# An RWKV attention with mixture-of-depths kernel: whole v tiles, quarter state products, and a new order of stores, weights and one batch's expert work

## The chip, the cores and the metric

The kernel runs on one core of one Trainium2 chip. The metric is the device time of one execution in microseconds (us). All times below come from three runs of the kernel before the change and from one profiled execution of it.

## The reference

The inputs r, k and v have 4 batches, 8 heads, 768 tokens and 48 channels a head. A decaying state runs over the tokens of each batch and head; its output y is then the input of a mixture-of-depths block, which sends the 128 best-scored tokens of each batch through a two-layer expert.

```python
for t in range(S):
    cur = einsum('bhd,bhe->bhde', u * k[t], v[t])
    y[t] = einsum('bhd,bhde->bhe', r[t], state + cur)
    state = w * state + einsum('bhd,bhe->bhde', k[t], v[t])
x = y as (B, S, H * D)                    # 4 x 768 x 384
scores = x @ w_gate
out = x
for b in range(B):
    top = the 128 tokens of batch b with the highest scores
    out[b, top] = x[b, top] + sigmoid(scores) * (relu(x[b, top] @ w1) @ w2)
```

w1 is 384 x 1024 and w2 is 1024 x 384. All is in float32.

## The kernel before

**Units.** A unit n is 128 tokens of one batch, so a batch has NC = 6 units and there are NU = 24. Within a unit two halves of C = 64 tokens are treated as chunks: inside a chunk the sum over earlier tokens is a masked matrix of scores (rows of the page: L259 scores, L302 the masked copy into `at`, L226 and L234 its diagonal), and between chunks a state of 48 x 48 a head is carried (Z0, Z1, G; `states` and `decays`). The output y of a unit is the sum of `from_state` (z times rh) and `from_values` (at times v); both are rows of L287.

**The main loop** (pass i, 0 to 24; its line numbers are in the listing) works on three units at once. On TensorE a pass issues, in this order: y from the states of unit i-1; the scores of unit i; in passes called *late* the state products of unit i (L269); y from the values of unit i-1; the transposes of k and r of unit i+1 (L240, into the PSUM tiles `pt` and `ea` or `st`); in passes not late the state products of unit i (L282, tile `st`); pieces of the expert's matrices if some are queued (`hidden` L467, `expert` L477); one transpose of a column of scores (L369); and, when no expert work is queued, three matmuls that nobody reads (L264), written into a part of the next unit's `rp` tile. A pass is late when the expert's queue is not empty at its start.

VectorE does the masked copy, the state sums, the product rh (L245), the bonus sum `du` (L219) and the ranks of tokens. ScalarE copies y out to x (L330, L331), copies k's transpose (L250), and makes the first half of the diagonal (L226) and the decays (L318). GpSimd (POOL) makes the second half of the diagonal (L234), then for unit i+2 the scaled k (`scaled`, L209) and the bonus products (`bonus`, L213 and L215), then what is to be gathered or scattered (L417, L508).

**The transfers.** All loads and the stores of x are issued by SP, in the order in which the loop writes them: in pass i k and r of unit i+4 (192 KB each, 1024 runs of 192 B), v of unit i+3 in two halves (96 KB each), `weights(WEIGHTS.get(i, 0))` pieces of w1 (128 KB) or w2 (192 KB), then the store of unit i-2. A store waits for ScalarE's copy of its unit. Both halves of v lie in one tile with a dimension of two chunks; what belongs to the other chunk is zero, so that one matmul over 128 tokens gives the state sums of both chunks side by side. The zeros are written once by `clear_v`, for each of the six v buffers, on POOL, ScalarE or VectorE.

**The expert's work.** When batch b's last unit e has left, pass e+3 ranks its tokens, makes a one-hot matrix, picks the 128 indices (`pick`, L405 and L409) and gathers their rows from the output in HBM (`fetch`, L417, by POOL). The gather waits for all stores of this batch. In pass e+4 `chosen` transposes the gathered rows (L434) and copies them (L436), and `enqueue` puts 8 pieces of `hidden`, 8 of `expert` and a `leave` into the queue; `share(i)` spreads them over the following passes. `at` places each of these at a named place of a pass, and `run` calls what stands there. The last batch is done after the loop.

The lines that hold the order are these:

```python
b, c = divmod(n, NC)                      # load_v: two halves
for j in range(2):
    rows = slice(c * T + j * C, c * T + (j + 1) * C)
    nc.sync.dma_start(out=vins[n % NV][half(j), :, j, :], in_=v[b, :, rows, :]...)
WEIGHTS = {i: 1 for i in range(3, 9)} | {9: 3, 10: 3, 11: 3, 12: 3, 13: 2}
```

Of the kernel before, what the change touches and what calls it, by code (L numbers as in the profile page):

```python
# [7 lines left out]
F32 = mybir.dt.float32  # L8
# [9 lines left out]
def kernel(  # L18
# [13 lines left out]
    nc = tc.nc  # L32
# [29 lines left out]
    nc.vector.memset(tiny, 0.0)  # L62
    zero = const.tile([128, 1], F32)
    nc.vector.memset(zero, 0.0)
    one = const.tile([1, 128], F32)
# [5 lines left out]
    kws = [const.tile([128, H, PAD], F32, name=f"kw{i}") for i in range(NKW)]  # L71
    vins = [const.tile([128, H, 2, D], F32, name=f"vin{i}") for i in range(NV)]
    KIN = {}

    def half(j):
        return slice(j * C, (j + 1) * C)
# [11 lines left out]
    def load_v(n):  # L88
        b, c = divmod(n, NC)
        for j in range(2):  # L90
            rows = slice(c * T + j * C, c * T + (j + 1) * C)
            nc.sync.dma_start(out=vins[n % NV][half(j), :, j, :], in_=v[b, :, rows, :].rearrange("h t d -> t h d"))

    def clear_v(n):
        for j in range(2):
            o = vins[n][half(j), :, 1 - j, :]
            if n in (2, 3):
                nc.scalar.activation(o, zero[half(j), :, None].to_broadcast([C, H, D]), AF.Copy)
            elif n == 4:
                nc.vector.memset(o, 0.0)  # L100
            else:
                nc.gpsimd.memset(o, 0.0)

# [10 lines left out]
    nc.scalar.activation(tiny[:, 1:2], tiny[:, 0:1], AF.Sigmoid)  # L114
    clear_v(2)
    clear_v(3)

# [13 lines left out]
    tri = const.tile([128, 128], F32)  # L131
    clear_v(4)
    up = const.tile([128, NP, C + 1], F32)
    nc.vector.memset(up[:, :, 0:1], 1.0)
    winv = const.tile([128, 1, NP], F32)

    clear_v(0)
    clear_v(1)
    nc.gpsimd.memset(rpads[1][:, :, D:], 0.0)  # L139
# [50 lines left out]

    WEIGHTS = {i: 1 for i in range(3, 9)} | {9: 3, 10: 3, 11: 3, 12: 3, 13: 2}
    parts = [(q, kd) for q in range(4) for kd in range(KD)] + list(range(FB))
# [12 lines left out]

    KH, RH, RKU, DU, AT, RP, ST, Z0, Z1, G, YP, YS, X = {}, {}, {}, {}, {}, {}, {}, {}, {}, {}, {}, {}, {}

# [53 lines left out]

    def unread(t, m):
        for _ in range(m):
            nc.tensor.matmul(out=t, lhsT=ident, rhs=ident, start=True, stop=True, skip_group_check=True)  # L264

    def state_product(n, hp, i, c):
        if c and n % NC == NC - 1:
            return
        nc.tensor.matmul(out=RP[n][half(i), c, NP * C + hp * D : NP * C + (hp + 1) * D],  # L269
                         lhsT=kws[n % NKW][half(c), 2 * hp + i, :], rhs=vins[n % NV][half(c), 2 * hp + i, c, :],  # L270
                         start=True, stop=True, skip_group_check=True)

    def sums(n, c):
        if n not in ST:
            return RP[n][:, c, NP * C : NP * (C + D)].rearrange("d (p e) -> d p e", p=NP)
        return ST[n][:, : NP * 2 * D].rearrange("d (p c e) -> d p c e", p=NP, c=2)[:, :, c, :]

    def state_products(n):
        m = 1 if n % NC == NC - 1 else 2
        for hp in range(NP):  # L280
            for i in range(2):
                nc.tensor.matmul(out=ST[n][half(i), hp * 2 * D : (hp * 2 + m) * D], lhsT=kws[n % NKW][:, 2 * hp + i, :],  # L282
                                 rhs=vins[n % NV][:, 2 * hp + i, :m, :], start=True, stop=True, skip_group_check=True)

# [12 lines left out]
    def from_values(n, hp, i, c):  # L297
        y_product(n, c, hp, i, AT[n][half(c), i * NP + hp, :], vins[n % NV][half(c), 2 * hp + i, c, :])

# [249 lines left out]
    for b in range(B - 1):  # L549
        e = b * NC + NC - 1  # L550
        at(e + 3, "start", rank, b)
        for z in range(NST):
            at(e + 3, "start", one_hot, b, z)
            at(e + 3, "pick" if b else "chosen", pick, b, z, "pt")
            at(e + 3, "fetch", fetch, b, z)
            at(e + 4, "chosen", chosen, b, z, "pt")
            at(e + 5, "middle", gate_sum, b, z)
            at(e + 6, "gate", gate, b, z)
            at(e + 4, "chosen", enqueue, b, z)

# [17 lines left out]
    def first():  # L578
        RP[0] = psum.tile([128, 2, 512], F32, name="rp")
        for hp in range(NP):  # L580
            for j in range(2):
                for c in range(2):
                    score_product(0, hp, j, c)
        turned(1, turn(rpads[1], "ea"))
        ST[0] = psum.tile([128, 512], F32, name="st")
        state_products(0)
        Z1[0] = work.tile([128, NP, D], F32, name="z1")
        nc.vector.tensor_copy(Z1[0], sums(0, 0))
        diagonals(0)
        masked(0)  # L590
        G[0] = work.tile([128, NP, D], F32, name="g")
        nc.vector.tensor_add(G[0], sums(0, 1), Z1[0])
        turned_k(1, turn(kws[1], "pt"))
        bonus_sum(1)
        diagonals(1)
        nc.vector.tensor_mul(wc, up[:, :, C], up[:, :, C])  # L596
        nc.vector.tensor_scalar(tri, jp, 0.0, None, op0=OP.is_lt)
        nc.scalar.copy(wg, spread(1, "eb"))
        scaled(2)
        bonus(2)  # L600

    for i in range(NU + 1):
        if i + 4 < NU:
            load_kr(i + 4)
        if i + 3 < NU:
            load_v(i + 3)
        weights(WEIGHTS.get(i, 0))
        if i > 1:
            store_y(i - 2)
        late = bool(queue)  # L610
        if not i:
# [14 lines left out]
        if i < NU:  # L626
            if i not in RP:
                RP[i] = psum.tile([128, 2, 512], F32, name="rp")
            for hp in range(NP):
                for j in range(2):  # L630
                    for c in range(2):
                        score_product(i, hp, j, c)
            if late:
                for hp in range(NP):
                    for c in range(2):
                        for j in range(2):
                            state_product(i, hp, j, c)
        else:
# [19 lines left out]
        run(i, "start")  # L658
        if late and i < NU:
            states(i)  # L660
        if i + 1 < NU:
            if i:
                turned_k(i + 1, turn(kws[(i + 1) % NKW], "pt"))
            turned(i + 1, turn(rpads[(i + 1) % NIN], "st" if late else "ea"))
        run(i, "turned")
        old = len(ready)
        leaving()
        if i < NU and not late:
            if i:
                ST[i] = psum.tile([128, 512], F32, name="st")  # L670
            state_products(i)
            states(i)
        m = share(i)
# [13 lines left out]
        if 2 <= i < NU:  # L687
            against_earlier(i - 2)
            score_row(i - 2, None if late or i != NC + 2 else "ea")
            against_own(i - 2)  # L690
        run(i, "last")
        if i + 1 < NU and not queue:
            RP[i + 1] = psum.tile([128, 2, 512], F32, name="rp")
            unread(RP[i + 1][:, 0, 384:], 3)
        run(i, "chosen")
# [3 lines left out]
        if i == 2:  # L699
            clear_v(5)  # L700
        if i == 4:
            numbers()
# [69 lines left out]
```

## Time and profile before

| what | value |
|---|---|
| runs, median (lowest to highest) | 173.16 us (173.14 to 176.85) |
| profiled execution | 172.11 us |
| its span, first to last instruction | 170.3 us |
| mean granted TensorE clock | 0.97 |
| PE busy | 149.1 us (88% of the span) |
| DVE, ACT, POOL busy | 110.4, 97.6, 103.9 us |
| transfers | 24.13 MB, 142 GB/s on average, 93% of the packets under 512 B |
| median time from issue to landing: r, k, v half, store | 5.0, 4.3, 4.0, 3.5 us |
| the same: w1 piece, w2 piece, gather | 3.4, 4.1, 3.7 us |

The profile is a record of one execution. It gives each engine's busy time, a row of 40 slices, the chain of work that ended last, the groups of instructions by source line with what ended the idle time before them, and a timeline of single instructions. PE is TensorE's matmuls, PEld its weight loads, DVE is VectorE, ACT is ScalarE, POOL is GpSimd, SP issues transfers. L234 is line 234. In the chain of waits a line is start, length and what; in the timeline it is start, length, engine, line, operation, what is written and read, the shapes, and in brackets the idle time before it with what ended it. "issue" stands for a wait whose cause the profile does not name.

### The profile page before, as it was taken

Reading aid. Unit: us, or ns where it says so; the run is one execution under the profiler, and the core shown is the slowest. Engines: PE = TensorE matmul, PEld = TensorE weight load, DVE = VectorE, ACT = ScalarE, POOL = GpSimd, SP = SyncE. Lnnn points to the kernel's source line nnn. Section 1 sums busy time; section 2 is a strip of 40 time slices with the busy share of each in tenths; the row PEclk is TensorE's granted clock in tenths of the full one; section 3 lists DMA queues with packets and bytes.
Section 4 is the critical chain, followed back from the end, with each engine's and each line's share of the span. In section 5 each row is a group of like instructions: output and inputs, shape, how many; then the busy total and the mean of one; then the engine's idle time right before and its main releaser. Section 6 shows DMA issues by size and latency. Waiting matters only on the chain.

```text
span 170.3 us, 8282 instructions
## 1 busy us (share of the span) xinstructions
PE 149.1 (88%) x3475; PEld 127.1 (75%) x3475; DVE 110.4 (65%) x315; ACT 97.6 (57%) x346; POOL 103.9 (61%) x138
## 2 busy tenths in 40 slices
PE   5899999999996189996979967999998998997990
PEld 3677888988884179996848766998787797756990
DVE  5679988888980354768378479666975796733000
ACT  6656888886757026475637754875676867401200
POOL 7999998997660792866562696986558331022022
PEclk9999999999999755999999999999999999999999
DMA  3999799866886997678898996898721112112000
GB/s 67 179 187 168 143 175 188 198 144 119 191 199 154 183 214 188 144 178 230 183 233 209 206 198 125 182 220 169 157 98 50 50 52 94 48 18 80 0 20 26
DMA packets 82197, 24.13 MB, mean 142 GB/s; under 512 B 76126, under 2 KB 81792, under 8 KB 82160
## 3 DMA queue, kind: packets, MB, share of 16 engines
q1 hardware_dynamic: 81612, 22.03, 61.7%
q0 software_dynamic: 544, 1.57, 3.0%
q8 instruction: 27, 0.44, 1.1%
q14 instruction: 10, 0.08, 0.2%
q10 hardware_dynamic: 4, 0.00, 0.0%
HBM read 18.09 MB, written 5.51 MB: 139 GB/s over the span
## 4 chain that ended last, share of the span: by engine, by line
PE 64%; DMA 12%; issue 9%; DVE 5%; POOL 4%; ACT 3%; POOLq 1%; SPq 0%; ACTq 0%; DVEq 0%
PE y L287 13%; DMA xr<-out_dram,idx 7%; PE ea L467 7%; PE rp L259 6%; PE eb L467 6%; PE pt L240 5%; DMA w<-in_moe_w_dram 5%; PE eb L477 5%; PE st L282 3%; PE rp L269 3%; PE rp L264 3%; PE ea L240 3%; PE st L240 3%; PE ea L477 2%; ACT at L226 1%
## 5 line engine op out<-in xcount | busy, mean ns | idle before, releaser
L302 DVE COPY_PREDICATED at<-mask,rp 128x512 f32<-128x512 uint32 x24 | 17.8, 741 | 29.1 <-ACT at L226 10.1
L234 POOL TENSOR_TENSOR at<-dia,du 128x256 f32<-128x256 f32 x20 | 15.4, 769 | 23.3 <-DVE du L219 11.1
L226 ACT ACTIVATE at<-dia,du 128x64 f32<-128x64 f32 x96 | 25.5, 336 | 1.8 <-DVE du L219 1.8
L209 POOL TENSOR_TENSOR kw<-kin,wk 128x384 f32<-128x384 f32 x23 | 24.8, 1076 | 1.6 <-DMA kin<-in_k_dram 0.8
L215 POOL TENSOR_TENSOR rku<-rk,ub 128x384 f32<-128x384 f32 x24 | 24.5, 1020 | 1.9
L213 POOL TENSOR_TENSOR rk<-rpad,kin 128x384 f32<-128x384 f32 x23 | 23.4, 1016 | 1.5 <-DMA rpad<-in_r_dram 1.5
L318 ACT ACTIVATE z<-g,wc 128x48 f32<-128x48 f32 x80 | 19.9, 319 | 0.4 <-DVE wc L596 0.4
L259 PE MATMUL rp<-rh,kh 48*64 48x64 f32 x768 | 18.4, 229 | 1.0 <-DVE at L302 0.4
L417 POOL DMA_INDIRECT xr<-out_dram,idx x4 | 4.1, 1032 | 21.9 <-DVE part L485 10.1
L287 PE MATMUL y<-vin,at 64*64 64x48 f32 x736 | 16.8, 223 | 0.4 <-issue 0.4
L240 PE MATMUL pt<-ident,kw 128*128 128x128 f32 x96 | 16.6, 298 | 0.5 <-POOL rpad L139 0.4
L287 PEld LDWEIGHTS y<-z,rh 48*64 48x64 f32 x672 | 13.3, 138 | 4.8 <-issue 2.6
L259 PEld LDWEIGHTS rp<-rh,kh 48*64 48x64 f32 x768 | 15.4, 142 | 1.9 <-issue 1.0
L287 PE MATMUL y<-z,rh 48*64 48x48 f32 x672 | 16.3, 227 | 0.3 <-ACT x L331 0.3
L330 ACT COPY x<-y 64x192 f32<-64x192 f32 x46 | 14.4, 314 | 2.5 <-PE y L287 1.1
L344 DVE SCALAR_TENSOR_TENSOR scr<-x,wg 128x384 f32<-128x384 f32 x24 | 15.3, 637 | 0.7 <-ACT x L330 0.4
L287 PEld LDWEIGHTS y<-vin,at 64*64 64x64 f32 x736 | 14.3, 138 | 0.6 <-issue 0.6
L477 PE MATMUL ea<-w,ht 128*128 128x384 f32 x32 | 12.1, 497 | 2.4 <-DMA w<-in_moe_w_dram 2.4
L250 ACT COPY kh<-pt 128x512 f32<-128x512 f32 x23 | 13.6, 590 | 0.8 <-PE pt L240 0.8
L467 PE MATMUL eb<-xt,w 128*128 128x128 f32 x96 | 12.5, 278 | 1.4 <-issue 1.3
L625 ACT COPY tiny<-y 1x4 f32<-1x4 f32 x23 | 3.6, 157 | 17.2 <-PE y L287 17.2
L219 DVE TENSOR_REDUCE du<-rku 128x8 f32<-128x384 f32 x24 | 13.0, 543 | 0.0
(159 smaller groups left out, 306.6 us busy)
## 6 DMA issues: line engine op xcount, KB each, us to landing
rpad<-in_r_dram SPq DMA_DIRECT2D x24, 192.0 KB, 5.0
vin<-in_v_dram SPq DMA_DIRECT2D x48, 96.0 KB, 4.0
out_dram<-x SPq DMA_DIRECT2D x24, 192.0 KB, 3.5
kin<-in_k_dram SPq DMA_DIRECT2D x23, 192.0 KB, 4.3
w<-in_moe_w_dram SPq DMA_DIRECT2D x12, 128.0 KB, 3.4
w<-in_moe_w_dram SPq DMA_DIRECT2D x8, 192.0 KB, 4.1
kw<-in_k_dram SPq DMA_DIRECT2D x1, 192.0 KB
xr<-out_dram,idx POOLq DMA_INDIRECT x4, 3.7
```

The costliest lines, as they stand in the source:

```text
L209: (nc.gpsimd if n else nc.vector).tensor_mul(kws[n % NKW][:, :, :D], KIN[n], wk)
L213: nc.gpsimd.tensor_mul(rk, rpads[n % NIN][:, :, :D], KIN[n])
L215: nc.gpsimd.tensor_mul(RKU[n], rk, ub)
L226: nc.scalar.activation(AT[n][:, j, :], dia, AF.Copy, scale=du[:, j : j + 1])
L234: eng.tensor_mul(AT[n][:, h:, :], dia[:, None, :].to_broadcast([128, H - h, C]), du[:, h:, None].to_broadcast([128, H - h, C]))
L240: nc.tensor.transpose(t[:, hp, :], x[:, 2 * hp : 2 * hp + 2, :], ident)
L259: nc.tensor.matmul(out=RP[n][s, i, hp * C : (hp + 1) * C], lhsT=KH[n][head(i), hp, s], rhs=RH[n][head(i), hp, s], start=True, stop=True, s ...
L287: nc.tensor.matmul(out=YP[n][i][half(c ^ i), hp * D : (hp + 1) * D], lhsT=lhsT, rhs=rhs, start=(c, i) not in started, stop=True, skip_grou ...
L302: nc.vector.copy_predicated(at, causal, RP[n][:, :, : NP * C].rearrange("s i (p t) -> s i p t", p=NP))
L318: nc.scalar.activation(Z0[n + 1][:, hp, :], G[n][:, hp, :], AF.Copy, scale=wc[:, hp : hp + 1])
L467: nc.tensor.matmul(out=PE[b, z][:, f % 4, :], lhsT=w1[:, d, f * 128 : (f + 1) * 128], rhs=XT[b, z][d], start=(d == 0), stop=(d == KD - 1))
L477: nc.tensor.matmul(out=pe[:, : cols.stop - cols.start], lhsT=HT[b, z][:, f, :], rhs=w2[:, f, cols], start=(f == 0), stop=(f == FB - 1))
```

## The change

The change has these parts:

- v is loaded in one transfer of 128 tokens into a tile without the dimension of two chunks, and `clear_v` with its zeros is gone.
- The state products are always the quarter products (64 tokens, one chunk), issued right after the scores, in pass 0 too; the tile `st` of state sums is gone, they lie in `rp`, and the transposes of r go to `st` in all passes from unit 1. The state sums therefore stand ahead of rh in VectorE's order.
- Of three unread matmuls of 128 columns one of 192 columns is left, and it writes to `ea` (in pass 8 to `pt`) and no longer to `rp`.
- The weights begin in pass 2, one piece earlier, and pass 13 has one less.
- The stores of the last two units of a batch stand ahead of the loads in their pass; the other stores stay behind loads and weights.
- For batch 0 `chosen` and `enqueue` move from the end of pass 9 to the place after the transposes of pass 10.
- `numbers`, which writes constants on POOL, moves from pass 4 to pass 2.

```diff
@@ -60,8 +60,6 @@
     tiny = const.tile([1, 1 + NP], F32)
     nc.vector.memset(wrow[:, :, D:], 1.0)
     nc.vector.memset(tiny, 0.0)
-    zero = const.tile([128, 1], F32)
-    nc.vector.memset(zero, 0.0)
     one = const.tile([1, 128], F32)
     nc.vector.memset(one, 1.0)
     spacer = const.tile([1, 1], F32)
@@ -69,7 +67,7 @@
 
     rpads = [const.tile([128, H, PAD], F32, name=f"rpad{i}") for i in range(NIN)]
     kws = [const.tile([128, H, PAD], F32, name=f"kw{i}") for i in range(NKW)]
-    vins = [const.tile([128, H, 2, D], F32, name=f"vin{i}") for i in range(NV)]
+    vins = [const.tile([128, H, D], F32, name=f"vin{i}") for i in range(NV)]
     KIN = {}
 
     def half(j):
@@ -87,19 +85,8 @@
 
     def load_v(n):
         b, c = divmod(n, NC)
-        for j in range(2):
-            rows = slice(c * T + j * C, c * T + (j + 1) * C)
-            nc.sync.dma_start(out=vins[n % NV][half(j), :, j, :], in_=v[b, :, rows, :].rearrange("h t d -> t h d"))
-
-    def clear_v(n):
-        for j in range(2):
-            o = vins[n][half(j), :, 1 - j, :]
-            if n in (2, 3):
-                nc.scalar.activation(o, zero[half(j), :, None].to_broadcast([C, H, D]), AF.Copy)
-            elif n == 4:
-                nc.vector.memset(o, 0.0)
-            else:
-                nc.gpsimd.memset(o, 0.0)
+        rows = slice(c * T, (c + 1) * T)
+        nc.sync.dma_start(out=vins[n % NV], in_=v[b, :, rows, :].rearrange("h t d -> t h d"))
 
     urow = const.tile([1, 2, Dm], F32)
     nc.scalar.dma_start(out=urow[:, 0, :], in_=bass.AP(tensor=u.tensor, offset=u.offset, ap=[[0, 1], [1, Dm]]))
@@ -112,8 +99,6 @@
         load_kr(n + 2)
     load_v(2)
     nc.scalar.activation(tiny[:, 1:2], tiny[:, 0:1], AF.Sigmoid)
-    clear_v(2)
-    clear_v(3)
 
     jp = const.tile([128, 128], F32)
     nc.gpsimd.iota(jp, pattern=[[1, 128]], base=0, channel_multiplier=-1, allow_small_or_imprecise_dtypes=True)
@@ -129,13 +114,10 @@
         nc.gpsimd.tensor_scalar(mask[rows], jp[rows, c * C : (c + 1) * C], 0.0, None, op0=OP.is_gt)
     causal = mask.bitcast(U32)[:, None, None, :].to_broadcast([128, 2, NP, C])
     tri = const.tile([128, 128], F32)
-    clear_v(4)
     up = const.tile([128, NP, C + 1], F32)
     nc.vector.memset(up[:, :, 0:1], 1.0)
     winv = const.tile([128, 1, NP], F32)
 
-    clear_v(0)
-    clear_v(1)
     nc.gpsimd.memset(rpads[1][:, :, D:], 0.0)
     nc.gpsimd.memset(kws[0][:, :, D:], 0.0)
     nc.gpsimd.memset(kws[1][:, :, D:], 0.0)
@@ -188,7 +170,7 @@
     for hp in range(NP):
         nc.scalar.activation(tr[:, hp, :C], up[:, hp, :C], AF.Copy, scale=winv[:, 0, hp : hp + 1])
 
-    WEIGHTS = {i: 1 for i in range(3, 9)} | {9: 3, 10: 3, 11: 3, 12: 3, 13: 2}
+    WEIGHTS = {i: 1 for i in range(2, 9)} | {9: 3, 10: 3, 11: 3, 12: 3, 13: 1}
     parts = [(q, kd) for q in range(4) for kd in range(KD)] + list(range(FB))
 
     def weights(n):
@@ -203,7 +185,7 @@
     sc = [const.tile([128, NC], F32, name=f"sc{b}") for b in range(B)]
     scr = const.tile([128, Dm], F32)
 
-    KH, RH, RKU, DU, AT, RP, ST, Z0, Z1, G, YP, YS, X = {}, {}, {}, {}, {}, {}, {}, {}, {}, {}, {}, {}, {}
+    KH, RH, RKU, DU, AT, RP, Z0, Z1, G, YP, YS, X = {}, {}, {}, {}, {}, {}, {}, {}, {}, {}, {}, {}
 
     def scaled(n):
         (nc.gpsimd if n else nc.vector).tensor_mul(kws[n % NKW][:, :, :D], KIN[n], wk)
@@ -259,28 +241,25 @@
         nc.tensor.matmul(out=RP[n][s, i, hp * C : (hp + 1) * C], lhsT=KH[n][head(i), hp, s],
                          rhs=RH[n][head(i), hp, s], start=True, stop=True, skip_group_check=True)
 
-    def unread(t, m):
-        for _ in range(m):
-            nc.tensor.matmul(out=t, lhsT=ident, rhs=ident, start=True, stop=True, skip_group_check=True)
+    def unread(t):
+        nc.tensor.matmul(out=t[:, : NP * D], lhsT=ident, rhs=ub.rearrange("t h d -> t (h d)")[:, : NP * D],
+                         start=True, stop=True, skip_group_check=True)
 
     def state_product(n, hp, i, c):
         if c and n % NC == NC - 1:
             return
         nc.tensor.matmul(out=RP[n][half(i), c, NP * C + hp * D : NP * C + (hp + 1) * D],
-                         lhsT=kws[n % NKW][half(c), 2 * hp + i, :], rhs=vins[n % NV][half(c), 2 * hp + i, c, :],
+                         lhsT=kws[n % NKW][half(c), 2 * hp + i, :], rhs=vins[n % NV][half(c), 2 * hp + i, :],
                          start=True, stop=True, skip_group_check=True)
 
+    def state_products(n):
+        for hp in range(NP):
+            for c in range(2):
+                for i in range(2):
+                    state_product(n, hp, i, c)
+
     def sums(n, c):
-        if n not in ST:
-            return RP[n][:, c, NP * C : NP * (C + D)].rearrange("d (p e) -> d p e", p=NP)
-        return ST[n][:, : NP * 2 * D].rearrange("d (p c e) -> d p c e", p=NP, c=2)[:, :, c, :]
-
-    def state_products(n):
-        m = 1 if n % NC == NC - 1 else 2
-        for hp in range(NP):
-            for i in range(2):
-                nc.tensor.matmul(out=ST[n][half(i), hp * 2 * D : (hp * 2 + m) * D], lhsT=kws[n % NKW][:, 2 * hp + i, :],
-                                 rhs=vins[n % NV][:, 2 * hp + i, :m, :], start=True, stop=True, skip_group_check=True)
+        return RP[n][:, c, NP * C : NP * (C + D)].rearrange("d (p e) -> d p e", p=NP)
 
     def y_product(n, c, hp, i, lhsT, rhs):
         started = YS.setdefault(n, set())
@@ -295,7 +274,7 @@
             y_product(n, c, hp, i, RH[n][head(i), hp, half(c)], z[head(i), hp, :])
 
     def from_values(n, hp, i, c):
-        y_product(n, c, hp, i, AT[n][half(c), i * NP + hp, :], vins[n % NV][half(c), 2 * hp + i, c, :])
+        y_product(n, c, hp, i, AT[n][half(c), i * NP + hp, :], vins[n % NV][half(c), 2 * hp + i, :])
 
     def masked(n):
         at = AT[n].rearrange("s (i p) t -> s i p t", i=2)
@@ -553,10 +532,11 @@
             at(e + 3, "start", one_hot, b, z)
             at(e + 3, "pick" if b else "chosen", pick, b, z, "pt")
             at(e + 3, "fetch", fetch, b, z)
-            at(e + 4, "chosen", chosen, b, z, "pt")
+            where = (e + 4, "chosen") if b else (e + 5, "turned")
+            at(*where, chosen, b, z, "pt" if b else "eb")
+            at(*where, enqueue, b, z)
             at(e + 5, "middle", gate_sum, b, z)
             at(e + 6, "gate", gate, b, z)
-            at(e + 4, "chosen", enqueue, b, z)
 
     def share(i):
         n = sum(f is not leave for f, _ in queue)
@@ -581,8 +561,7 @@
             for j in range(2):
                 for c in range(2):
                     score_product(0, hp, j, c)
-        turned(1, turn(rpads[1], "ea"))
-        ST[0] = psum.tile([128, 512], F32, name="st")
+        turned(1, turn(rpads[1], "st"))
         state_products(0)
         Z1[0] = work.tile([128, NP, D], F32, name="z1")
         nc.vector.tensor_copy(Z1[0], sums(0, 0))
@@ -599,15 +578,18 @@
         scaled(2)
         bonus(2)
 
+    def next_store(i, ahead):
+        if i > 1 and ahead == ((i - 2) % NC >= NC - 2):
+            store_y(i - 2)
+
     for i in range(NU + 1):
+        next_store(i, True)
         if i + 4 < NU:
             load_kr(i + 4)
         if i + 3 < NU:
             load_v(i + 3)
         weights(WEIGHTS.get(i, 0))
-        if i > 1:
-            store_y(i - 2)
-        late = bool(queue)
+        next_store(i, False)
         if not i:
             first()
             continue
@@ -630,11 +612,7 @@
                 for j in range(2):
                     for c in range(2):
                         score_product(i, hp, j, c)
-            if late:
-                for hp in range(NP):
-                    for c in range(2):
-                        for j in range(2):
-                            state_product(i, hp, j, c)
+            state_products(i)
         else:
             against_earlier(i - 2)
             score_row(i - 2, "y")
@@ -656,20 +634,15 @@
         if i < NU:
             masked(i)
         run(i, "start")
-        if late and i < NU:
+        if i < NU:
             states(i)
         if i + 1 < NU:
             if i:
                 turned_k(i + 1, turn(kws[(i + 1) % NKW], "pt"))
-            turned(i + 1, turn(rpads[(i + 1) % NIN], "st" if late else "ea"))
+            turned(i + 1, turn(rpads[(i + 1) % NIN], "st"))
         run(i, "turned")
         old = len(ready)
         leaving()
-        if i < NU and not late:
-            if i:
-                ST[i] = psum.tile([128, 512], F32, name="st")
-            state_products(i)
-            states(i)
         m = share(i)
         if i < NU and m and (i, "pick") in fill:
             pieces(min(m, 2))
@@ -686,19 +659,16 @@
             pieces(m)
         if 2 <= i < NU:
             against_earlier(i - 2)
-            score_row(i - 2, None if late or i != NC + 2 else "ea")
+            score_row(i - 2, "ea" if i == NC + 2 else None)
             against_own(i - 2)
         run(i, "last")
         if i + 1 < NU and not queue:
-            RP[i + 1] = psum.tile([128, 2, 512], F32, name="rp")
-            unread(RP[i + 1][:, 0, 384:], 3)
+            unread(psum.tile([128, 512], F32, name="pt" if i == NC + 2 else "ea"))
         run(i, "chosen")
         if i + 2 < NU:
             scaled(i + 2)
             bonus(i + 2)
         if i == 2:
-            clear_v(5)
-        if i == 4:
             numbers()
         send(old)
         run(i, "fetch")
```

## The prediction

> **What bounds the kernel now.** I read the slices, then the chain of waits in order of time, then the timeline of the transfers' issuing queue (SP) against the compute engines, then stage windows. The whole chain names TensorE (64%), and a unit without expert pieces is a closed row of matmuls:
>
> ```profile
> 26.39 0.61 PE y L287 x32
> 27.00 0.48 PE rp L259 x32
> 27.48 0.53 PE y L287 x32
> 28.01 0.59 PE pt L240 x4
> 28.60 0.44 PE ea L240 x4
> 29.04 0.81 PE st L282 x16
> 29.85 0.25 PE eb L369
> 30.10 0.67 PE rp L264 x6
> ```
>
> These eight pieces make 4.38 us, and the next unit's y starts at 30.77: no hole. But the transfers are slower than that. SP issues from 0.75 to 122 us almost without a gap, 5.2 to 5.6 us a unit after the start, and the units catch up with it. The rows to look at are who waits for whom in units 8 and 9 (unit i is the loop's pass i):
>
> ```profile
> 46.34 1.01 POOL L209 TENSOR_TENSOR kw<-kin,wk 128x384 f32<-128x384 f32 x1 [0.85 <-DMA kin<-in_k_dram]
> 48.87 1.00 POOL L213 TENSOR_TENSOR rk<-rpad,kin 128x384 f32<-128x384 f32 x1 [1.53 <-DMA rpad<-in_r_dram]
> ...
> 52.69 0.38 SPq L335 DMA_DIRECT2D out_dram<-x  x1
> ...
> 56.31 1.18 POOL L417 DMA_INDIRECT xr<-out_dram,idx  x1 [5.01 <-issue]
> ...
> 58.18 0.73 DVE L302 COPY_PREDICATED at<-mask,rp 128x512 f32<-128x512 uint32 x1 [7.42 <-POOL at L234]
> ...
> 58.96 1.65 PE L264 MATMUL rp<-ident 128*128 128x128 f32 x6 [5.24 <-DVE at L302]
> ```
>
> First: at 46 to 49 us k and r of unit 10 are used the moment they land; the loads' lead is gone. Second: the gather of batch 0 has its index at 50.8 and stands in POOL's queue until 56.31. It needs batch 0's last store, whose x ACT finished at 38.06, but which SP issued at 52.69, behind 14 us of queued transfers; landing takes 3.5 (page, part 6). Behind the gather stands L234, behind that the masked copy, behind that TensorE. "issue" hides this wait. What follows is seen in windows (columns: stretch, its length, busy time of PE, PEld, DVE, ACT and POOL, granted clock, DMA share, GB/s):
>
> ```profile
> 51.00:59.00 8.00, 2.76 (x66) 2.23 (x58) 0.82 (x2) 3.40 (x13) 2.95 (x5) 0.92 0.81 164
> 59.00:70.00 11.00, 10.56 (x179) 9.70 (x181) 6.88 (x20) 4.19 (x15) 7.10 (x9) 0.59 0.79 184
> 70.00:80.00 10.00, 9.45 (x287) 8.96 (x279) 7.09 (x22) 7.59 (x27) 6.88 (x8) 1.00 0.82 202
> 80.00:90.00 10.00, 8.17 (x258) 6.23 (x258) 5.12 (x15) 4.95 (x21) 6.52 (x8) 1.00 0.86 203
> ```
>
> The 5.24 us of idle TensorE are followed by 11 us at 0.59 of its clock. Third, w2 comes late, and batch 1's gather too:
>
> ```profile
> 80.97 0.88 PE L477 MATMUL ea<-w,ht 128*128 128x384 f32 x2 [1.52 <-DMA w<-in_moe_w_dram]
> 87.14 0.91 PE L477 MATMUL ea<-w,ht 128*128 128x384 f32 x2 [0.86 <-DMA w<-in_moe_w_dram]
> 99.43 0.52 PE L434 MATMUL pt<-ident,xr 128*128 128x128 f32 x3 [1.69 <-DMA xr<-out_dram,idx]
> ```
>
> After 122 us the DMA share is 0.16: the last 48 us are computation alone.
>
> **The change, part by part.** Starts of y(i), the state matmuls that open pass i, measure progress: before, y(9) 49.9, y(10) 61.9, y(11) 69.8, y(12) 75.0, y(13) 81.9, y(14) 88.1, y(15) 93.2, y(16) 99.9.
>
> *Zeros and start.* Twelve clears go: POOL four of 0.41 (3.01 to 4.77), ACT 2.1, DVE 0.88. The first transposes start at 5.05, when k(0) lands (issued 1.66), and the next at 6.20 with r(0): 0 gained. The later pair of POOL (0.88 at 21.95) makes room for numbers(), moved two passes earlier (0.81+0.17+0.17+0.11 less overlap): 0.
>
> *State products and unread matmuls.* Quarter products replace the 0.81 row of L282; the same work in units with pieces is the L269 row, 0.38 to 0.45: 0.36 saved a unit (0.60 to about 0.3 for a batch's last). Unread: 384 columns took 0.67, 192 take 0.33 (between 0.25, L369's one matmul, and 0.67). Together 0.7 in each of passes 1 to 8, 5 us of TensorE work. DVE now does the two state sums (0.36 each) ahead of rh; scores need rh at y+4.3, it is ready at about y+4.2: 0. What hides the 5 us is the loads. For pass i, r(i+1) must land, then POOL does L213 1.0, L215 1.07, L234 0.8, and the masked copy starts 2.0 after y(i); so y(i) is at least the landing of r(i+1) + 0.9. By issue + 5.0 (median landing, part 6) r(4) to r(9) land 0.5 to 1.9 before their L213, so those passes can be that much earlier and then wait; r(10), issued 43.67, lands with its L213 and gives y(9) = 49.6. Gain at y(9): 0.3. If loads were no limit, 5.
>
> *v in one transfer.* The same 8 x 128 runs of 192 B, one issue less. From above: if SP's own issuing were the limit, 0.60 a unit (the second vin row's least time). From below: 0; a k, an r and two v halves come 3.3 us apart per unit in the start, about 1.1 for each 192 KB, halves or not. SP's vin pair swells from 1.5 to 3.3 us though the buffers' last readers are long done, so I read the queue as full and the transfers behind it as the pace: 0.13, near the lower end. [...] These rows show two halves issued in 1.85, so it overlaps, and the row decides: 1.8 us.
>
> *Weights.* One more at pass 2 (128 KB, about 0.6) puts all later loads back 0.6, and each group of weights starts one piece further on. Net with the above: transfers of 65 to 95 us land 1.2 earlier (ends: 0.6 later, 7 earlier).
>
> *Stores ahead.* Stores 4, 5 (10, 11, 16, 17) pass k, r, v and weights of one pass in SP's queue. Store 5 goes to the place of the k at 47.77 and lands at 51.3. Each costs the loads behind it 0.38 of issue and up to 0.9 of transfer; r(10) comes 0.6 later, which with +0.6 of weights and 10 x 0.13 of v cancels. POOL, with its L215 done at 50.8, issues the gather at 51.3 (1.0 to 1.2), L234 (0.62) ends at 53.0, the masked copy (0.73) at 53.75, the sum for Z1 (0.35) at 54.1. Unread matmuls no longer need rp, so nothing of TensorE stands behind the masked copy but y(10), at 54.2: 7.7 earlier, 7.4 of it here. If the store were late as before, 0 of this.
>
> *chosen and enqueue of batch 0* go one place later: three transposes (0.52 at full clock) after pass 10's turns; then ACT's xt copy 0.48, behind kh, which ends 4.4 after y (69.77 to 74.2). TensorE ends its turns at y+3.05 and gets xt at y+4.95, the transposes within that wait: pass 10 takes 5.25 + 1.9 = 7.15. Before it took 7.9 at the low clock. y(11) = 61.4, 8.4 earlier. r(12), issued 53.65, allows 59.6.
>
> *What is late next: weights.* Passes take 5.25 at full clock. Weights land 3.4 (w1) or 4.1 (w2) after issue, less 1.2. Pass 12 (66.7) needs the last quarter of w1 at 69.8, which lands at 71.5 (issued 70.35 less the shift): wait 1.8; then w2's first at about 74: wait 1.3. y(13) = 75.0. Pass 13 needs the three w2 of 76.27 at 78.1, has them at 79.6 to 80.7: 1.5; y(14) = 81.7. Pass 14: 0.5 (82.93); y(15) = 87.3. Pass 15: the w2 of 89.47 at 92.1, 1.3; batch 1's gather is no longer late, its 1.69 goes. y(16) = 93.5: 6.35 earlier. r(17), issued 86.59, allows 92.5. The rest is as before.
>
> **Sum.** 0.3 (early passes) + 7.4 (gather) + 0.7 (pass 10) - 1.4 - 0.5 - 0.5 (weights, passes 12 to 14) + 0.35 (pass 15) = 6.35. Span 170.3 to 163.95; the profiled execution took 172.11, 1.8 more than its span, and the median is 173.16. I subtract from the median: 166.8.
>
> The rule that speaks against this is in TensorE: Matmul & The Clock Gate, "HAM oscillation": matmul pauses over some 3.4 us bring the half clock. Rows: after 5.24 idle 0.59, after 1.52 and 0.86 idle 1.00. My new waits, 1.8 and 1.3 in pass 12, stay under it; if they merged into one over 3.4, an episode like 59 to 70 would cost some 4.5 and the time would be 171.3.
>
> **Rivals.** (A) One transfer for v makes the stream itself quicker, near 0.6 a unit: weights stop waiting, y(16) at 87 to 90. For it: vin's second issue never falls under 0.60. Against: SP stands in the first half too, up to 2.9 us. 160 to 163.5. (B) Merging brings nothing, so the transfers land 0.6 later instead of 1.2 earlier and weights wait 1.8 longer: 168.6; with the clock fallen too, up to 171.5. For it: 12 weight transfers are issued between 61 and 84 us. (C) Slower: with fewer unread matmuls TensorE has holes of up to 1.5 us in each early unit; if the clock falls for passes 2 to 9, 3.7 us of work become 7.4 against a load pace of 5.2: 2.2 x 8 = 17.6, less 6.3: 184. It decides once the granted share stays under 0.7 there. Against: 1.00 in 80 to 90 us with such holes. (D) It doesn't do what it says: store 5 lands after 55 and the gather stands as before: 172 to 174.
>
> **Numbers.** Likeliest 0.52 (own range 164 to 169), A 0.22, B 0.14, C 0.07, D 0.05. About 2% can be told from no change here. Faster: 0.52 + 0.22 + 0.05 of B = 0.79; same 0.14 (the rest of B, D); slower 0.07. Range 160.5 to 170.5 leaves out C, D and the ends of A and B.
>
> **What would show it.** Right: gather issued within 1.5 us of its index, no slice under 0.9 in the clock row, y(10) near 54, y(9) hardly earlier than 49.9, L467 and L477 waiting for w by some 5 us in passes 12 to 15, SP still without gaps. Wrong: L213 no longer at the landing of r (then loads were not the limit, A), or w waits above 3 us each with a clock dip (B).

## The result, and the profile after

The changed kernel took 167.19 us in the median of four runs (165.80 to 172.15) against 175.00 (173.14 to 177.00); the ratio is 0.964, 95% interval 0.954 to 0.975: 4.4 to 7.9 us of 173.16. In a second set of runs (experiments 1 to 4 below) it was 170.09 (168.41 to 171.92) against 175.81 (170.67 to 178.71). Some executions of every kernel are a few per cent slower than its others; the ratios, and the times given for experiments 1 to 4, are of the faster ones, and as before has only one of these in the second set, 170.67, that set alone does not show the gain again.

Its first profiled execution took 172.15, above the 165.8 to 167.8 of its other runs, so I read a second one (169.51, span 167.7, experiment 1). No execution near 166 has a profile.

The page of that second execution: the slices of TensorE and of its clock, the instruction queue, and two groups.

```profile
PE   5897578869589959899999999969998999997990
...
PEclk9999999978957995999999999999999999999997
...
q8 instruction: 28, 0.46, 1.3%
...
L266 PE MATMUL y<-vin,at 64*64 64x48 f32 x736 | 18.6, 227 | 8.5 <-issue 6.0
...
L195 POOL TENSOR_TENSOR rk<-rpad,kin 128x384 f32<-128x384 f32 x23 | 23.5, 1021 | 0.0
```

Before, the slices from 9 to 50 us had TensorE at 9 and its clock at 9. Now TensorE has 5 to 9 there, and the clock falls twice between 34 and 56 us. L195 (L213 before) never waits for r: idle 0.0 where it was 1.5. The waits of TensorE, longest first (columns: in total, times, longest):

```profile
PE y L266 <- issue: 6.0, 5, 1.7
PE y L266 <- POOL rk L195: 2.5, 1, 2.5
PE pt L222 <- issue: 1.7, 1, 1.7
```

No row names a transfer of w any more; before there were 2.4 us of them. The gather of batch 0, in order of time:

```profile
58.08 0.15 DVE L388 TENSOR_REDUCE idx<-pt 128x1 int32<-128x2 f32 x1
...
58.52 1.18 POOL L396 DMA_INDIRECT xr<-out_dram,idx  x1 [3.53 <-DMA out_dram<-x]
...
60.39 0.73 DVE L281 COPY_PREDICATED at<-mask,rp 128x512 f32<-128x512 uint32 x1 [2.16 <-POOL at L216]
...
61.47 0.59 PEld L266 LDWEIGHTS y<-z,rh 48*64 48x64 f32 x32 [1.69 <-ACT kh L232]
```

It is issued 0.29 us after its index instead of 5 us later, and the next pass follows: the wait that I called the second point is gone. (The store that the row names as its releaser is the profile's inference: store 5 had landed at 49.5.) But the index itself is ready at 58.2, where it was 50.8. So I set the passes side by side. The table gives the length of each stage in us, from the starts of y(i) on TensorE; "predicted" is my working, the last four columns are experiments 2, 3, 5 and 7 below.

| stage | before | predicted | changed | 2 | 3 | 5 | 7 |
|---|---|---|---|---|---|---|---|
| start to y(9) | 49.9 | 49.6 | 56.3 | 50.0 | 57.5 | 51.0 | 48.4 |
| y(9) to y(10) | 11.9 | 4.6 | 5.2 | 7.1 | 5.0 | 5.2 | 5.2 |
| y(10) to y(11) | 7.9 | 7.2 | 8.4 | 6.6 | 7.1 | 7.2 | 10.4 |
| y(11) to y(12) | 5.2 | 5.3 | 5.2 | 6.0 | 5.2 | 5.3 | 5.6 |
| y(12) to y(13) | 6.9 | 8.3 | 5.4 | 11.2 | 5.4 | 10.3 | 5.4 |
| y(13) to y(16) | 18.0 | 18.5 | 16.3 | 18.8 | 16.3 | 20.0 | 16.6 |
| y(16) to end | 70.4 | 70.5 | 70.9 | 71.4 | 73.1 | 70.7 | 71.1 |
| span | 170.3 | 164.0 | 167.7 | 171.1 | 169.6 | 169.7 | 162.7 |

The total came out near the forecast; the stages did not. Passes 1 to 8 lost 6.4 us, pass 9 won 6.7, passes 12 to 15 won 3.2 where I had put a loss of 1.9. At y(10) the changed kernel stands at 61.5 and before at 61.9, at y(12) at 75.1 and 75.0: in this execution the whole gain in the span, 2.6 us, comes behind y(12).

**Where passes 1 to 8 lose.** TensorE in the second profile of the changed kernel, in order of time:

```profile
29.77 0.56 PE L266 MATMUL y<-vin,at 64*64 64x48 f32 x23 [1.14 <-issue]
...
33.09 0.26 PE L266 MATMUL y<-vin,at 64*64 64x48 f32 x2
...
33.16 0.43 PE L266 MATMUL y<-vin,at 64*64 64x48 f32 x10
35.23 0.55 PE L266 MATMUL y<-vin,at 64*64 64x48 f32 x20 [1.64 <-issue]
35.71 1.11 PE L222 MATMUL pt<-ident,kw 128*128 128x128 f32 x4
...
44.08 0.28 PE L266 MATMUL y<-vin,at 64*64 64x48 f32 x2
46.84 1.10 PE L266 MATMUL y<-vin,at 64*64 64x48 f32 x30 [2.48 <-POOL rk L195]
47.86 1.11 PE L222 MATMUL pt<-ident,kw 128*128 128x128 f32 x4
```

A row of 32 equal matmuls stops in the middle, after 2 + 10 or after 2, and goes on. All 32 read the same two tiles, and the first of them had run. "POOL rk" is the releaser that the profile inferred; these matmuls do not read rk. The stops are at matmul 345, 472, 598, 724 and 976 of the program: 126 or 127 apart, or twice that. With its weight load each matmul is two instructions, so 126 are 252. The instruction queue q8 made 28 transfers of 16 KB; TensorE's 2 x 3583 instructions over 28 are 256 (before: 2 x 3475 over 27, 257). From the trace, the transfer of q8 beside each stop:

```
stop at matmul   q8 transfer starts, takes   TensorE stands
345              17.89, 1.21                 19.00 to 20.70
472              22.75, 0.98                 23.89 to 25.02
598              27.23, 0.93                 28.63 to 29.77
724              32.69, 1.11                 33.59 to 35.23
976              44.53, 0.96                 44.36 to 46.84
```

So I read the stops as the end of one page of instructions (one such transfer of 16 KB), which TensorE reaches before the next has come. Then the clock, in stretches of 2 us (columns: stretch, length, busy time of PE, PEld, DVE, ACT, POOL, granted clock, DMA share, GB/s):

```profile
32.00:34.00 2.00, 1.59 (x88) 1.47 (x80) 1.96 (x9) 1.49 (x8) 1.29 (x2) 1.00 1.03 203
34.00:36.00 2.00, 0.77 (x22) 0.72 (x23) 0.82 (x2) 0.72 (x4) 1.92 (x3) 0.94 0.50 102
36.00:38.00 2.00, 2.00 (x10) 2.00 (x9) 0.29 (x1) 1.44 (x5) 0.47 (x1) 0.50 0.84 210
...
44.00:46.00 2.00, 0.36 (x22) 0.23 (x14) 1.97 (x7) 1.46 (x7) 2.00 (x3) 1.00 1.09 208
46.00:48.00 2.00, 1.16 (x31) 1.07 (x32) 0.24 (x1) 0.01 (x1) 1.30 (x2) 0.50 0.31 67
48.00:50.00 2.00, 2.00 (x10) 2.00 (x11) 0.13 (x1) 1.52 (x4) 0.00 (x0) 0.50 0.84 221
```

After the stops of 1.64 and 2.48 us TensorE runs at half its clock, which lengthens the next rows (four transposes of 0.66 take 1.11).

### The profile page after: what moved, and what is told of

It reads as the page before. It is cut to its first block, busy times and chain, and to the rows that moved or that the text cites. A ratio compares the mean times of both kernels' runs of the same rounds, so it can differ in the third digit from the quotient of the medians.

```text
span 170.3 us, 8426 instructions
## 1 busy us (share of the span) xinstructions
PE 152.0 (89%) x3583; PEld 129.8 (76%) x3583; DVE 108.3 (64%) x312; ACT 96.2 (56%) x342; POOL 100.0 (59%) x132
## 4 chain that ended last, share of the span: by engine, by line
PE 80%; issue 7%; ACT 4%; DMA 4%; DVE 1%; POOLq 1%; POOL 1%; SPq 0%; ACTq 0%; DVEq 0%
PE y L266 17%; PE pt L222 9%; PE rp L241 8%; PE rp L251 7%; PE st L222 7%; PE ea L446 7%; PE eb L446 7%; PE eb L456 5%; PE ea L456 4%; PE ea L245 2%; DMA kw<-in_k_dram 2%; DMA xr<-out_dram,idx 2%; PE eb L348 1%; ACT at L208 1%; ACT z L297 1%
## 5 line engine op out<-in xcount | busy, mean ns | idle before, releaser
L266 PE MATMUL y<-vin,at 64*64 64x48 f32 x736 | 19.8, 233 | 5.2 <-issue 5.2
L195 POOL TENSOR_TENSOR rk<-rpad,kin 128x384 f32<-128x384 f32 x23 | 23.0, 1001 | 0.0
L227 DVE TENSOR_TENSOR rh<-st,tr 128x512 f32<-128x512 f32 x23 | 15.8, 685 | 9.0 <-PE st L222 8.9
L266 PEld LDWEIGHTS y<-vin,at 64*64 64x64 f32 x736 | 17.0, 148 | 5.7 <-issue 5.6
L241 PE MATMUL rp<-rh,kh 48*64 48x64 f32 x768 | 20.3, 241 | 1.0 <-issue 0.8
L251 PE MATMUL rp<-vin,kw 64*64 64x48 f32 x704 | 18.4, 231 | 2.7 <-issue 2.7
L222 PE MATMUL pt<-ident,kw 128*128 128x128 f32 x96 | 18.7, 324 | 1.1 <-issue 0.9
L266 PEld LDWEIGHTS y<-z,rh 48*64 48x64 f32 x672 | 14.5, 150 | 6.0 <-issue 1.7
L251 PEld LDWEIGHTS rp<-vin,kw 64*64 64x64 f32 x704 | 16.3, 149 | 3.3 <-issue 3.0
L241 PEld LDWEIGHTS rp<-rh,kh 48*64 48x64 f32 x768 | 17.1, 152 | 2.0 <-issue 1.6
L222 PE MATMUL st<-ident,rpad 128*128 128x128 f32 x92 | 16.2, 305 | 0.0
```

The source lines that it names most:

```text
L195: nc.gpsimd.tensor_mul(rk, rpads[n % NIN][:, :, :D], KIN[n])
L222: nc.tensor.transpose(t[:, hp, :], x[:, 2 * hp : 2 * hp + 2, :], ident)
L227: nc.vector.tensor_mul(RH[n], pr, tr)
L241: nc.tensor.matmul(out=RP[n][s, i, hp * C : (hp + 1) * C], lhsT=KH[n][head(i), hp, s], rhs=RH[n][head(i), hp, s], start=True, stop=True, s ...
L266: nc.tensor.matmul(out=YP[n][i][half(c ^ i), hp * D : (hp + 1) * D], lhsT=lhsT, rhs=rhs, start=(c, i) not in started, stop=True, skip_grou ...
```

## The experiments

My theory after the result: the changed kernel has more TensorE instructions a pass and less work in each, so it waits for pages (passes 1 to 8), and the stream of loads is well ahead of it. The rivals: loads are the pace, as I predicted; TensorE's work is the pace; the transfers of data hold up the pages.

**1. The changed kernel once more.** No edit.

> The changed kernel once more, for a second profile. In the first one TensorE stands still in the middle of rows of equal matmuls (2.20 us at 25.44, 2.36 at 36.79, 2.40 at 52.55), always some 126 matmuls or a multiple of that after the last such place, beside a 16 KB transfer of the instruction queue, and the granted clock falls after it. Theory 1 (the page of instructions comes late, by chance of the transfers around it): the places stay at the same multiples, the length and number of the stalls differ from execution to execution; with fewer of them the span is 163 to 166. Theory 2 (the stalls have nothing to do with instructions, something waits for data): same stalls at the same places again, span near 170.

Measured: 169.51 (168.41 to 170.68). Theory 1 holds: stops at 345, 472 and 724 as in the first profile, others (598, 976) in place of 1102, lengths between 1.13 and 2.48; the span, 167.7, is above the 163 to 166 that I named.

**2. Before, with only the stores moved.**

```diff
+    def next_store(i, ahead):
+        if i > 1 and ahead == ((i - 2) % NC >= NC - 2):
+            store_y(i - 2)
...
+        next_store(i, True)
         if i + 4 < NU:
             load_kr(i + 4)
...
-        if i > 1:
-            store_y(i - 2)
+        next_store(i, False)
```

> The kernel before with nothing changed but the order in SP's queue: the last two stores of a batch go ahead of the loads. My prediction puts 7.4 us of the 6.35 on this one step; with v in two halves and the old clears the loads behind come up to 1 us later, and weights wait: 165 to 169. Rival (the store alone is worth little, since the wait moves on to weights and loads that come later): 171 to 174.

Measured: 172.48 (172.05 and 172.90) beside the one 170.67 of before: no gain, and not the 165 to 169 of my prediction. The gather's row says that the step itself works:

```profile
52.18 1.17 POOL L417 DMA_INDIRECT xr<-out_dram,idx  x1 [0.81 <-issue]
```

Its wait was 5.01; pass 9 is 4.8 us shorter. And the waits of TensorE say where that went:

```profile
PE ea L477 <- DMA w<-in_moe_w_dram: 3.2, 2, 2.9
...
PE eb L467 <- DMA w<-in_moe_w_dram: 1.6, 1, 1.6
```

Before, the waits for w were 2.4 in all; here, too, the clock's slices between 77 and 86 us are at 5 and 7. By y(12) 5.3 us are won, by y(13) 1.0 is left: the rival of this experiment holds. Alone, the step on which I had put most of the gain is worth little here.

**3. The changed kernel with all stores behind the loads.**

```diff
-        if i > 1 and ahead == ((i - 2) % NC >= NC - 2):
+        if i > 1 and not ahead:
```

> The changed kernel with every store behind its pass's loads, as before. If the store order is what counts: 170 to 174, the gather of batch 0 waits about 5 us again. If fewer products and one transfer for v have brought the stream forward by themselves, store 5 lands early anyway and the time stays within 165 to 168.

Measured: 171.47 (171.34 and 171.60), 2.0 above experiment 1. The time lies in the first of the two ranges, but not for its reason: the gather does not wait for the store.

```profile
58.80 1.18 POOL L396 DMA_INDIRECT xr<-out_dram,idx  x1 [5.78 <-PE y L266]
```

Store 5 is issued at 47.73 and lands at 52.45, six us before the gather; TensorE has no wait for xr but the 1.0 at the end of the span. So the 5 us did not come back, since y(9) was late (57.5), and pass 9 took 5.0 as in experiment 1. The profile has page stops of 2.68 at 49.7 and 2.57 at 109.0; what makes the medians differ is not settled.

**4. The changed kernel with v in two transfers.**

```diff
-        rows = slice(c * T, (c + 1) * T)
-        nc.sync.dma_start(out=vins[n % NV], in_=v[b, :, rows, :].rearrange("h t d -> t h d"))
+        for j in range(2):
+            rows = slice(c * T + j * C, c * T + (j + 1) * C)
+            nc.sync.dma_start(out=vins[n % NV][half(j)], in_=v[b, :, rows, :].rearrange("h t d -> t h d"))
```

> The changed kernel with v in two transfers of 96 KB, as before, into the same tile without zeros. My prediction gives one transfer for v 0.13 us a unit: 24 units, of which some 14 lie where loads or weights bind: +0 to +2 us on the changed kernel, 166 to 169. Rival A (SP's issuing is the pace, 0.6 a unit): +5 to +8, 172 to 175, and the w2 waits of passes 12 to 15 are back.

Measured: 170.58 (169.90 and 171.25), 1.1 above experiment 1: within my 0 to +2, far from rival A's 5 to 8, and the ranges overlap. Its profile, of an execution of 177.15, has no wait for w, so the w2 waits that rival A named are not back; but TensorE was late there too (y(12) at 78.7). This does not settle what one transfer is worth.

**5. Before, with all but v in one transfer, quarter products and one unread matmul:** experiment 2, with the new weights table and batch 0's chosen rows one pass later. (`numbers` stays in pass 4, so it is not quite all the rest.)

```diff
-    WEIGHTS = {i: 1 for i in range(3, 9)} | {9: 3, 10: 3, 11: 3, 12: 3, 13: 2}
+    WEIGHTS = {i: 1 for i in range(2, 9)} | {9: 3, 10: 3, 11: 3, 12: 3, 13: 1}
...
-            at(e + 4, "chosen", chosen, b, z, "pt")
+            where = (e + 4, "chosen") if b else (e + 5, "turned")
+            at(*where, chosen, b, z, "pt" if b else "eb")
+            at(*where, enqueue, b, z)
```

> The kernel before (wide state products, three unread matmuls, v in two halves with zeros) with all the rest of the change: last stores ahead, weights spread anew, batch 0's chosen rows one pass later. New theory (pages): quarter products make TensorE run through its 16 KB instruction pages in 3.4 us where a page takes 4.3 to 5.4 to come, so the changed kernel loses 6 to 10 us in passes 2 to 9 (its y(9) at 56.3 and 59.9 against 49.9 before) which it wins elsewhere. Then this kernel has no stalls in the middle of equal matmuls before pass 9 and y(9) near 50; with the gather gone and weights partly late (2 to 4 us) 163 to 170, no slower than the changed kernel. Rival (the narrow v and the quarter products are needed to bring weights in time): y(9) near 50 but over 5 us of waits for w, 170 to 173.

Measured, in a third set of runs (experiments 5 to 8): 171.68 beside 174.02, ratio 0.987 (0.976 to 0.999). As the page theory has it, no stop before pass 9 and y(9) at 51.0. Its time, though, is the rival's: "no slower than the changed kernel" failed. TensorE's waits in it:

```profile
PE ea L477 <- DMA w<-in_moe_w_dram: 3.0, 2, 2.5
...
PE eb L467 <- DMA w<-in_moe_w_dram: 2.2, 2, 1.7
```

**6. The changed kernel with three narrow unread matmuls a pass.**

```diff
-        nc.tensor.matmul(out=t[:, : NP * D], lhsT=ident, rhs=ub.rearrange("t h d -> t (h d)")[:, : NP * D],
-                         start=True, stop=True, skip_group_check=True)
+        for _ in range(3):
+            nc.tensor.matmul(out=t[:, : NP * D], lhsT=ident, rhs=ub.rearrange("t h d -> t (h d)")[:, : NP * D],
+                             start=True, stop=True, skip_group_check=True)
```

> The changed kernel with three of its unread matmuls where it has one: 0.66 us more of TensorE work a pass in passes 1 to 8, 4 more instructions of some 270. Pages theory: the work goes into the time in which TensorE waits for a page anyway; stalls in passes 2 to 8 are shorter by about 0.5 each, fewer fall over 2 us, the clock falls less: -3 to +1 us on the changed kernel. If TensorE's work is the pace there: +4 to +5.

Measured: 170.05 beside 174.02, ratio 0.978 (0.969 to 0.987). The edit adds four matmuls and four weight loads a pass, 8 instructions and not 4. In its profile, of an execution of 173.77, the stops in passes 2 to 4 are 1.15, 0.88 and 1.02, the clock does not fall before 60 us, and y(9) is at 55.1: 0.66 us more of work in each pass did not make it later than the 56.3 and 59.9 of the changed kernel's two profiles. Whether the whole is slower than the changed kernel (0.964, in another set of runs) by 0 or by 2 us isn't told by these runs.

**7. The changed kernel with half of from_state left out in passes 2 to 8:** 16 matmuls and 16 weight loads a pass go.

```diff
-                for j in range(2):
+                for j in range(1 if 2 <= i <= 8 else 2):
                     for q in (1, 0):
                         from_state(i - 1, hp, j, q)
```

> The changed kernel with half of the state matmuls that open passes 2 to 8 left out (16 of 32, 32 of some 270 instructions a pass, 0.3 us of TensorE work): that part of the output of those units is not computed. Pages theory: 12% fewer pages in those passes, 0.5 to 0.6 us a pass earlier on top of no change elsewhere, y(9) 3 to 5 us earlier than in the second profile of the changed kernel (56.3): 51 to 53. If loads are the pace of these passes, as I predicted: y(9) unchanged within 1 us, and L195 begins at the landing of r.

Measured: 165.51 beside 174.02, ratio 0.951 (0.939 to 0.962). Its clock row, and a row of TensorE's waits:

```profile
PEclk9996899999999995999999999999999999999997
```

```profile
PE y L266 <- issue: 0.6, 2, 0.4
```

Those 0.6 us were 6.0, and between 20 and 60 us the clock does not fall. The work left out is 7 x 0.34 = 2.4 us (half of a row of 0.68); y(9) came 7.9 us earlier. Together with experiment 6, where more work with hardly more instructions cost nothing, this is the clearest sign that what counts here is the number of instructions. Loads were not the pace: y(9) would not have moved. In whole executions the step is smaller: 0.951 beside 0.971 of experiment 8, which has the changed kernel's instructions, is 3.5 us, and beside the changed kernel's 0.964 some 2, no more than the work left out, with intervals that overlap. After y(10) it meets one page stop of 2.17 at 57.26 (pass 10: 10.4), and it has no wait for w at all.

**8. The changed kernel without v's loads in passes 3 to 8.**

```diff
-        if i + 3 < NU:
+        if i + 3 < NU and not 3 <= i <= 8:
             load_v(i + 3)
```

> The changed kernel without the loads of v in passes 3 to 8 (those units take an older v, so their output is not the reference's): 1.1 MB less in 20 to 55 us, instructions of TensorE the same. If a page comes late because the data transfers stand before it: page stalls in passes 4 to 9 mostly gone, y(9) at 48 to 52. If a page takes its 4 to 5 us whatever else is moved: y(9) stays at 54 to 58. If loads are the pace (as predicted), y(9) is earlier by up to 1.1 a pass with L195 no longer at the landing of r.

Measured: 168.62 (168.36 to 172.34) beside 174.02, ratio 0.971 (0.963 to 0.979): no gain over the changed kernel. Its profile, of the 172.34, has the stops at 345, 472, 724 and 1102 again, one of them 3.18 us long, from 34.6; the DMA engines were 0.42 busy from 36 to 44 us, and y(9) is at 58.6. In this execution less data to move did not bring the pages sooner; and a load-bound pass would have gained.

## Why the prediction came out, point by point

*Loads hide the shorter passes (0.3 at y(9)).* This step failed, and so did its sign: 6.4 us were lost. I priced quarter products and unread matmuls by their time and not by their number. Counted in the traces, a middle pass of before has 127 matmuls in 4.38 us: 4.35 us for 126. The changed one has 139 in 3.77 where nothing stops it (experiment 3, pass 6): 3.4 us for 126. Experiment 7 has 123 in 3.87 to 4.67 in passes 2 to 7 (some 4.0 or more for 126), and no stop over 0.4 there. So somewhere between 3.4 and 4.0 us for 126 matmuls TensorE overtakes its instructions here. r(10) landed at 47.5 in the second profile, which by my own rule allowed y(9) at 48.4; it was 56.3.

"If loads were no limit, 5" was too much as well. Experiment 7 has neither page stops nor a wait for loads in these passes, and less work, and its y(9) is 1.5 earlier than before. GpSimd is the nearest limit there: its four rows of a pass take 3.8 and follow one another from 29 to 48 us with 0.3 us of idle time.

```profile
32.23 0.82 POOL L216 TENSOR_TENSOR at<-dia,du 128x256 f32<-128x256 f32 x1
33.01 1.00 POOL L191 TENSOR_TENSOR kw<-kin,wk 128x384 f32<-128x384 f32 x1
33.97 1.01 POOL L195 TENSOR_TENSOR rk<-rpad,kin 128x384 f32<-128x384 f32 x1
35.06 1.00 POOL L197 TENSOR_TENSOR rku<-rk,ub 128x384 f32<-128x384 f32 x1
```

*The clock.* I took the rule of some 3.4 us from the Trainium skill (TensorE: Matmul & The Clock Gate, "HAM oscillation") as a margin: pauses of 1.3 to 1.8 would not bring it down. Here the clock fell after stops of 1.42, 1.64 and 2.48, while it did not after 1.13 and 1.70; the measurement decides, a pause of 1.4 us is no safe one, and its length alone does not tell. Rival C saw a fallen clock in these passes and named the unread matmuls, but took it for a lasting state (17.6 us); it came as episodes of 3.4 and 6.8 us.

*The gather (7.4).* The size came out, 6.7 in this stage, but in this execution not by the order of the stores: experiment 3, with the old order, has 5.0 for pass 9 too, since where the early passes are late the store is landed in time in either order. Where they are punctual, the order does it: 4.8 in experiment 2, 6.7 in experiment 5, where the chosen rows have left pass 9 as well. So the mechanism is right for kernels near the one before; in the profiled changed kernel the late passes hide it.

*The chosen rows one place later (0.7).* Not seen in the changed kernel: pass 10 took 8.4 where 7.2 was forecast, at a clock of 0.79 from 62 to 70 us. Experiment 5 has the 7.2.

*Weights (-2.4, less 0.35).* Failed: no wait for w where I had put 6.4 in passes 12 to 15 (1.8, 1.3, 1.5, 0.5 and 1.3). Two things may do it. TensorE is late, so the weights are not; and the stream may be quicker than I sized it. Experiments 5 (v in halves) and 7 (one transfer) reach y(12) at about the same time, 68.7 and 69.7, and have 5.2 us of waits for w against none. From r(4) to r(10) the landings took 29.9 to 31.0 us in the four profiles with v in halves (before and experiments 2, 4, 5) and 25.5 to 29.3 in the five with one transfer (the changed kernel twice and experiments 3, 6, 7): 0.1 to 0.9 a unit, where I had 0.13 and rival A 0.60. The only pair that differs in nothing but v, experiments 4 and 1, has 29.9 and 29.3, 0.1 a unit, with TensorE late in both. The direction is rival A's in all nine, but how much of it is v's is open.

*The sum.* 6.35 was forecast; the ratio makes it 6.2 (4.4 to 7.9), the one profiled execution 2.6. In that execution two errors stand against each other, 6.7 us at y(9) and 5.1 in passes 12 to 15; pass 9, pass 10 and the end add 2.1. How much of the first error the executions near 166 have is not recorded. So the total came out by compensation, which is luck. Of the signs that I had named for being right, the gather's came (0.29 us after its index); the clock row (it has a 5), y(10) near 54 (61.5), y(9) hardly earlier (6.4 later) and the waits for w (none) did not, and L195 no longer at the landing of r was my sign of being wrong.

Not tried: wide products up to unit 8, where TensorE outruns its pages, and v in one transfer with quarter products from unit 9 on. Experiments 5 and 7 point to it, and its gain is open. Nor is settled what sets the time of a page.

## What to carry to other kernels

Where TensorE runs many small matmuls, count its instructions per microsecond beside its busy time: here a shorter pass with more instructions was slower. A stop in the middle of a row of equal matmuls, put down to "issue" or to an engine that the row doesn't read, and at equal distances in the program, was here the end of a page of instructions. And a forecast whose total is right is not thereby understood: compare it stage by stage.

## What the hardware showed that I had not expected

A page of 16 KB came so late that TensorE stood 1.1 to 2.5 us at its boundary, with TensorE resuming 1.3 to 1.6 us after the transfer's end (33.80 to 35.23, 45.49 to 46.84). The Trainium skill (Runtime: NRT & Kernel Launch, "Instruction fetch mechanics") has the same 256 instructions to a block, and calls the cost of crossing it mostly hidden; here five crossings between 15 and 50 us were not. The kernel before shows such a stop too, its 1.27 us of "issue" at 103.43 beside a transfer of q8 at 102.28; in passes 1 to 8, at 4.35 us for 126 matmuls, it has none.
